# A fixed TensorE order, narrow matmuls gathered into one run per chunk, full-height passes and a reordered front in an mLSTM kernel with attention experts

## The chip, the cores and the metric

The kernel runs on one core of a Trainium2 chip. The metric is device time of one execution in microseconds (us), lower is better. Five engines work side by side: TensorE (PE; its weight loads are shown apart as PEld), VectorE (DVE), ScalarE (ACT), GpSimd (POOL) and SyncE (SP), whose queue issues nearly all DMAs. They wait for each other through semaphores only.

## The reference

Two stages follow each other. The first is an mLSTM with scalar gates for 4 batches x 8 heads, 768 steps, head size 40. The second is a mixture of 4 causal attention experts of size 64 on the result, of which each row uses the best two.

```python
# B, H, S, D = 4, 8, 768, 40
for t in range(S):
    m_new = max(f[t] + m, i[t]); f_stab = exp(f[t] + m - m_new); i_stab = exp(i[t] - m_new); m = m_new
    C = f_stab * C + i_stab * outer(v[t], k[t])
    n = f_stab * n + i_stab * k[t]
    y[t] = sigmoid(o[t]) * (C @ q[t]) / max(abs(n . q[t]), 1)
x = y as (4, 768, 320)
w = softmax of the 2 largest of x @ w_gate, 0 for the others
for e in range(4):
    q, k, v = x @ wq[e], x @ wk[e], x @ wv[e]          # 320 -> 64
    a = softmax(causal(q @ k.T / 8))
    out += w[:, e] * (a @ v @ wo[e])                   # 64 -> 320
```

Inputs and outputs are float32.

## The kernel before

**The mLSTM** is worked in 24 chunks of 128 steps (`chunks`, 6 per batch), each of two halves of T = 64 steps. `gates` (L148) makes the running maxima and cumulated decays of all steps on VectorE with scans. The cumulated log decays G go to DRAM as `gd` and come back, repeated over partitions, as the tile `dm` of each chunk (`load_dm`, L267). For chunk 0 alone (`npe` = 1) PE builds that tile with matmuls of one identity column (L303). `p1_prep` (L281) turns `dm` into the decay matrix with a mask, a bias and an exponential, and makes `ks`, keys times decay, on GpSimd. Then each chunk has four sets of sixteen narrow matmul records, all with 64 or 40 output columns of the array:

- `psc` (L344, `p1_intra`): keys times queries. The queries come as `qbd`, a tile with two heads side by side on a block diagonal, with zeros elsewhere.
- `pdc` (L377, `p1_state`): `ks` times values, the two state increments. VectorE adds them to the decayed state `cd`: `sts` (L402).
- `py` (L409): decayed scores times values.
- `pi` (L424): queries times the states. VectorE then multiplies by exp(G) (`yi`, L434) and adds `py` (L440).

The denominator, the output gate (a tanh) and the product follow on VectorE and ScalarE, and `p1_out` (`px`, L467) transposes the chunk into `xh` and `xl`: a rounded high part for fast passes and the remainder.

Each chunk loads `kqs` (keys and queries, 2 DMAs of 160 KB), `qbd` (2 of 80 KB), `dm` (2 of 128 KB) and `nat` (keys, values, output gate by rows, 648 KB).

**The experts** are worked in 8 units (`units`: batch, half of 384 rows), `part2` at L494. The weights are split into high and low parts too (`split_weights`, L234), so a projection is eight passes (`passes`): high times high, low times high, high times low for the first 256 features, and for the last 64 features one pass over 128 rows (high and low weights stacked) and one pass over 64 rows, `WH[0:64]` with `xl[0:64]`. `queries`, `keys` (L527, 384 columns, four projections a unit) and `values` (L540, 260 columns, three a unit) use them. `queries` writes `QD` and `QL`, `keys` writes `KS`; both go through SP-queue DMAs that copy halves to other partitions.

`scores` (L599) takes, per expert and 128 rows, a pass with `QD` over 128 rows (L611) and a pass with `QL` over 64 rows (L614), in pieces of at most 512 columns. Row block i of half hf has N = (3 hf + i + 1) x 128 columns, so the pieces have 512, 384, 256 or 128 columns: 48, 16, 32 and 32 pairs. VectorE adds the causal mask in place in PSUM and takes the row extreme (L623); ScalarE reads PSUM and writes the exponential to `A` (L633). `flip` (L657) transposes `A` on PE, and ScalarE or VectorE copies it to `AT`. `mix` (L718) multiplies `AT` with the values (64 array columns, L742) and scales by `R`, which goes through DRAM (`fd`). `project` (L758) does the output projection. The last unit works by rows (`flip_rows`, `mix_rows`).

**The order of the work.** Every helper is a generator that yields the estimated PE time of what it has just emitted. `merge` draws from three streams of a unit by weights `ca`, `cb`, `c0`/`c1`: three chunks of the mLSTM six chunks ahead, the next unit's projections, and the unit's scores, flips and mix. A helper can thus be interrupted at each yield: `psc` in four places, `pdc`, `py` and `pi` likewise, and between the passes of a projection. The framework's planner then orders every engine's list by its own estimates and by priorities (`later`, `off`), except where `keep_in_program_order` binds an instruction. The front (from L839) loads chunks 0 to 2 and the weights, keeps PE's clock up with two groups of 16 dummy matmuls (`warm`, L86), and goes through the first five steps of the chunk list before the streams start.

```python
    for n in range(5):
        st = seq1[n][:1] if n == 0 else seq1[n]
        for _ in chain(st):
            pass
```

PSUM has two large buffers (`big`: dummy matmuls and scores) and four of one bank (`one`) for everything else.

## Time and profile before

| | us |
|---|---|
| median of 3 runs | 429.44 |
| lowest and highest of them | 426.6, 430.35 |
| span of the profiled execution, first to last instruction | 430.9 |
| PE busy in it | 406.9 (94%) |
| VectorE, ScalarE, GpSimd busy | 272.4, 199.3, 122.4 |
| mean granted TensorE clock | 0.939 of full |

The profiled execution has no other time of its own than its span, which lies 1.5 us above the median of the runs. The profile's busy time of PE counts matmuls that overlap in a pipeline. How densely they follow each other is read from the starts in the timeline. "Idle before" in brackets is the time that an engine stood still ahead of an instruction, and what ended it.

### The profile page before, as it was taken

The page shows a single profiled execution, that of the slowest core. Times are in us where ns is not written, and L with a number is a line of the kernel's source. Part 1 is how long each engine was busy: PE and PEld are TensorE (multiplying, and loading weights), DVE is VectorE, ACT ScalarE, POOL GpSimd, SP SyncE. Part 2 cuts the span into 40 slices and gives each one's busy share as a digit, 9 for nine tenths or more (in the row PEclk, how much of TensorE's full clock was granted, in tenths as well). Part 3 has the DMA queues.
Part 4 walks back from the last instruction along what each step waited for, and adds up shares of the span by engine and source line. Part 5 has one row for each costly group of instructions (what it writes and reads, how often), then busy time and mean ns, then how long its engine had stood idle before and what let it go on. Part 6 is the DMA issues. An engine that isn't in the chain of part 4 may idle for free.

```text
span 430.9 us, 9143 instructions
## 1 busy us (share of the span) xinstructions
PE 406.9 (94%) x3202; PEld 289.6 (67%) x3202; DVE 272.4 (63%) x844; ACT 199.3 (46%) x561; POOL 122.4 (28%) x157
## 2 busy tenths in 40 slices
PE   6975599899999999999999999999999999989996
PEld 2664478666676776677667767676768766755675
DVE  8686977946967683557746684567766633443552
ACT  1336323434444566336354565344445744543473
POOL 7336533432524523223544043240220000000000
PEclk9785889959989999999999999999999999986999
DMA  6998968755577752446745663255212221420010
GB/s 190 247 223 204 203 187 210 147 150 147 157 192 188 206 153 55 97 138 182 221 95 144 173 185 76 55 185 151 57 42 72 69 56 40 108 65 20 20 44 30
DMA packets 44429, 55.85 MB, mean 130 GB/s; under 512 B 5824, under 2 KB 38816, under 8 KB 44384
## 3 DMA queue, kind: packets, MB, share of 16 engines
q1 hardware_dynamic: 44192, 55.08, 48.7%
q8 instruction: 25, 0.41, 0.4%
q14 instruction: 20, 0.16, 0.1%
q10 hardware_dynamic: 192, 0.20, 0.1%
HBM read 38.59 MB, written 4.07 MB: 99 GB/s over the span
## 4 chain that ended last, share of the span: by engine, by line
PE 81%; DMA 12%; DVE 3%; SPq 1%; ACT 1%; issue 1%; ACTq 0%
PE pp L527 12%; PE sc L614 10%; PE pt L657 10%; PE pa L742 8%; PE sc L611 8%; PE pv L540 7%; PE po L763 6%; PE psc L344 5%; DMA dm<-gd 5%; PE pi L424 3%; DMA qbd<-in_kq 3%; PE py L409 3%; PE pdc L377 3%; DMA kqs<-in_kq 2%; PE pt L679 2%; PE px L467 2%
## 5 line engine op out<-in xcount | busy, mean ns | idle before, releaser
L623 DVE CUSTOM_DVE_ANT_0 sc<-sc,maskw 128x128 f32<-128x128 f32 (+5 forms) x96 | 59.7, 637 | 42.4 <-PE sc L614 38.7
L522 ACT ACTIVATE AT<-pt 128x128 f32<-128x128 f32 (+2 forms) x137 | 49.4, 395 | 53.5 <-PE pt L657 43.5
L633 ACT ACTIVATE A<-sc,nmx 128x128 f32<-128x128 f32 (+5 forms) x96 | 61.0, 636 | 28.0 <-DVE nmx L623 25.5
L611 PE MATMUL sc<-KS,QD 128*128 128x512 f32 (+3 forms) x128 | 52.5, 417 | 1.2 <-ACT A L633 1.1
L614 PE MATMUL sc<-KS,QL 64*128 64x512 f32 (+3 forms) x128 | 53.0, 426 | 0.0
L657 PE MATMUL pt<-cst,A 128*128 128x128 f32 x276 | 48.7, 293 | 0.7 <-DVE dm L356 0.7
L344 PE MATMUL psc<-qbd,kqs 104*64 104x128 f32 x384 | 32.1, 308 | 7.9 <-DMA kqs<-in_kq 3.4
L742 PE MATMUL pa<-AT,V 128*64 128x384 f32 (+2 forms) x240 | 39.1, 423 | 0.0
L657 PEld LDWEIGHTS pt<-cst,A 128*128 128x128 f32 x276 | 31.0, 144 | 11.1 <-issue 2.9
L402 DVE TENSOR_TENSOR sts<-pdc,cd 40x164 f32<-40x164 f32 x80 | 25.9, 324 | 19.2 <-PE pdc L377 18.1
L614 PEld LDWEIGHTS sc<-KS,QL 64*128 64x128 f32 x128 | 23.4, 188 | 21.3 <-issue 15.8
L394 POOL TENSOR_TENSOR cd<-sts,dec 104x328 f32<-104x328 f32 x30 | 22.4, 747 | 52.1 <-DVE sts L402 31.4
L527 PE MATMUL pp<-xl,WH 128*128 128x384 f32 (+1 forms) x96 | 37.0, 385 | 0.0
L527 PE MATMUL pp<-xh,WH 128*128 128x384 f32 x96 | 36.8, 383 | 0.2 <-ACT xh L470 0.2
L611 PEld LDWEIGHTS sc<-KS,QD 128*128 128x128 f32 x128 | 24.4, 194 | 17.9 <-issue 11.5
L756 POOL TENSOR_TENSOR yl<-yf,yh 128x384 fp32r<-128x384 f32 x14 | 14.0, 1003 | 78.9 <-ACT yh L753 78.9
L323 POOL TENSOR_TENSOR dm<-dm,cst 128x512 f32<-128x512 f32 x18 | 23.2, 1290 | 35.9 <-DMA dm<-gd 27.6
L344 PEld LDWEIGHTS psc<-qbd,kqs 104*64 104x64 f32 x384 | 24.2, 152 | 12.8 <-issue 7.5
L742 PEld LDWEIGHTS pa<-AT,V 128*64 128x64 f32 x240 | 18.2, 138 | 14.9 <-issue 12.0
L327 POOL TENSOR_TENSOR ks<-nat,dm 128x320 f32<-128x320 f32 x24 | 18.9, 788 | 27.8 <-PE pdc L377 11.9
L424 PE MATMUL pi<-sts,kqs 104*64 104x82 f32 x384 | 23.4, 249 | 2.6 <-DVE xl L471 1.6
L377 PE MATMUL pdc<-nat,ks 128*40 128x82 f32 x352 | 23.5, 252 | 1.2 <-DVE kl L593 0.9
(133 smaller groups left out, 789.7 us busy)
## 6 DMA issues: line engine op xcount, KB each, us to landing
nat<-in_nat SPq DMA_DIRECT2D x24, 648.0 KB
kqs<-in_kq SPq DMA_DIRECT2D x48, 160.0 KB
QD<-qh SPq DMA_DIRECT2D x64, 96.0 KB
dm<-gd SPq DMA_DIRECT2D x46, 128.0 KB
qbd<-in_kq SPq DMA_DIRECT2D x48, 80.0 KB
out<-ob SPq DMA_DIRECT2D x24, 160.0 KB
KS<-kh SPq DMA_DIRECT2D x32, 96.0 KB
KS<-kl SPq DMA_DIRECT2D x32, 96.0 KB
```

The costliest lines, as they stand in the source:

```text
L344: ins = nc.tensor.matmul(pv[a * T : (a + 1) * T, g, :, sub, :], kc[:, 2 * g + a, sub * T : (sub + 1) * T], qb[:, 2 * g + a, :, sub * T : ( ...
L377: nc.tensor.matmul(pdc[z * 64 : z * 64 + D, o : o + 2 * D1], ks[:, sub, 2 * g + z, :], v1[:, sub, 2 * g + z, :], start=True, stop=True,)
L424: nc.tensor.matmul(piv[sub * T : (sub + 1) * T, g, :, a, :], qc[:, 2 * g + a, sub * T : (sub + 1) * T], sin[sub][:, 2 * g + a, :, :], star ...
L522: nc.scalar.activation(o, x, AF.Copy)
L527: nc.tensor.matmul(pp[:, :HALF], w(slice(mt * P, (mt + 1) * P)), x(slice(0, HALF)), start=(n == 0), stop=(n == len(ps) - 1),)
L540: nc.tensor.matmul(pv[:, : E * HD + E], x(slice(i * P, (i + 1) * P)), w(slice(NQK, NW)), start=(n == 0), stop=(n == len(ps) - 1),)
L611: nc.tensor.matmul(sc[:, o + c0 : o + c1], QDs[p][:, ee, ts], KS[:, e, c0:c1], start=True, stop=False)
L614: nc.tensor.matmul(sc[:, o + c0 : o + c1], QLs[p][r0 : r0 + 64, ts], KS[r0 : r0 + 64, e, c0:c1], start=False, stop=True,)
L623: nc.vector.tensor_tensor_reduce(out=sc[:, o : o + N], in0=sc[:, o : o + N], in1=maskw[:, S - N : S], scale=1.0, scalar=3e38, op0=ALU.add, ...
L633: nc.scalar.activation(A[:, n * HALF : n * HALF + N], sc[:, o : o + N], AF.Exp, bias=nmx, scale=-1.0, accum_out=zs[:, i, e : e + 1],)
L657: nc.tensor.transpose(pt[:, (s - s0) * P : (s - s0 + 1) * P], A[:, c : c + P], ident)
L742: nc.tensor.matmul(pa[ee * 64 : ee * 64 + 64, c0:HALF], kvs[(b, s // 3)][:, s % 3, e * HD : (e + 1) * HD], ATs[e][:, aoff(s) + c0 : aoff(s ...
```

## The change

PE's list is written out by the program and kept (`manual_schedule` for PE); for the front this holds for all engines. The planner's priorities and most of the tuning table go.

- `narrow(n)` emits for one chunk all of `psc` and `pdc` (a new helper `p1_inc`), the `mix` matmuls that stand asked for, and `py` and `pi` of the chunk before, without interruption, then the loads of chunk n+2 and the preparation of chunk n+1. `flow` calls it at even distances of an own clock `clk` and fills the time between with the projections, scores, flips and output projections. A helper that by this clock would still wait for another engine yields `None`, and the next one is taken.
- The `QL` pass and the last `xl` pass of a projection take 128 rows. `QL` becomes a tile per expert with zeros in the other 64 rows, written in two halves by VectorE.
- Queries are multiplied by exp(G) ahead (`p1_scale`, GpSimd). exp(G) goes to DRAM as `ge` and comes back as `eqs` by two DMAs of 96 KB a chunk. `pi` is added to `py` in one bank by PE, and `yi` with its two VectorE operations goes. The denominator starts with an Abs on ScalarE; the copy of the last 64 features moves from GpSimd to VectorE.
- The loads of `kqs` and `qbd` have 48 rows in place of 40: 2 DMAs of 192 and 2 of 96 KB.
- `dm` comes from PE for chunks 0 to 5, with the mask added by PE. For chunks 0 to 2, `qbd` is filled from `kqs` by ScalarE (`spread`) instead of by DMA.
- The masked scores are written to `A` in SBUF, where `exp` works in place. `A` gets four buffers, `ob` three.
- The front: one group of dummy matmuls, gates in three parts between the first chunks, weights behind the loads of chunk 0 to 2, `split_weights` behind chunk 2, then the first two `values` of unit 0. Chunks 3, 4 and 5 come after it.

```diff
+    ctx.enter_context(tc.manual_schedule(engines={mybir.EngineType.PE}))
...
         r += [
             (lambda c: WH[:, 2, c], lambda t: xh[:, 2, t]),
-            (lambda c: WH[0:64, 2, c], lambda t: xl[0:64, 2, t]),
+            (lambda c: WH[:, 2, c], lambda t: xl[:, 2, t]),
         ]
...
+    def p1_scale(b, j):
+        qc = kqs[(b * NCH + j) % len(kqs)][:, 1]
+        nc.gpsimd.tensor_tensor(qc, qc, eqs[(b * NCH + j) % len(eqs)], op=ALU.mult)
...
-        piv = pi[:, : H * D1].rearrange("p (g c a d) -> p g c a d", g=2, c=2, a=2)
+        piv = py[:, : H * D1].rearrange("p (z g a d) -> p g z a d", g=2, z=2, a=2)
         for g in range(2):
             for a in range(2):
-                for sub in range(2):
+                for sub in range(j == 0, 2):
                     nc.tensor.matmul(
                         piv[sub * T : (sub + 1) * T, g, :, a, :],
                         qc[:, 2 * g + a, sub * T : (sub + 1) * T],
                         sin[sub][:, 2 * g + a, :, :],
-                        start=True,
-                        stop=True,
+                        start=False,
+                        stop=g == 1 and a == 1,
                     )
...
-        yi = p2.tile([P, H, D1], F32, tag="yi", name=f"yi_{nm}")
-        nc.vector.tensor_tensor(
...
-        nc.vector.tensor_tensor(yi, pyv, yi, op=ALU.add)
...
         def queries(p):
+            slot = (2 * u + p) % len(qls)
+            while qlu[slot]:
+                yield None
             pq = yield from proj(2 * p)
...
-            nc.vector.scalar_tensor_tensor(QL, pq, -0.125, qh.bitcast(F32), op0=ALU.mult, op1=ALU.subtract)
+            for ee in range(2):
+                r = slice(ee * 64, ee * 64 + 64)
+                nc.vector.scalar_tensor_tensor(
+                    QL[r, ee, :], pq[r], -0.125, qh[r].bitcast(F32), op0=ALU.mult, op1=ALU.subtract
+                )
...
         def scores(es, i):
+            while clk[0] < kr.get((u, es[0] // 2), 1e9):
+                yield None
...
                     nc.tensor.matmul(
                         sc[:, o + c0 : o + c1],
-                        QLs[p][r0 : r0 + 64, ts],
-                        KS[r0 : r0 + 64, e, c0:c1],
+                        QLs[p][:, ee, ts],
+                        KS[:, e, c0:c1],
                         start=False,
                         stop=True,
                     )
...
                 nc.vector.tensor_tensor_reduce(
-                    out=sc[:, o : o + N],
+                    out=A[:, n * HALF : n * HALF + N],
...
+    def narrow(n):
+        c = 0.2
+        if 0 <= n < NC:
+            drive(p1_intra(*chunks[n]))
+            drive(p1_inc(*chunks[n]))
+            c += 1.53
+        for g in asked:
+            c += sum(g)
+        asked.clear()
+        if 3 <= n - 1 < NC:
+            drive(p1_state(*chunks[n - 1]))
+            c += 1.15
+        if 0 <= n and n + 2 < NC:
+            p1_load(*chunks[n + 2])
+        if 0 <= n and n + 1 < NC:
+            p1_prep(*chunks[n + 1])
+            p1_scale(*chunks[n + 1])
+        return c
...
+        while any(x[2] for x in live) or runs or (last and (asked or pend)):
+            if pend and (clk[0] >= pend[0][0] or idle > 20):
+                idle = 0
+                out()
+                continue
+            if (runs and (clk[0] >= nxt or idle > 6)) or (asked and not runs):
+                if pend:
+                    out()
+                idle = 0
+                nxt = run()
+                continue
...
+            st[0] += c
+            clk[0] += c
...
+        drive(p1_intra(0, 0))
+        gates_out(P, 3 * P)
+        decays(0, 6)
         load_weights(0)
...
+        load_weights(1)
+        nc.sync.dma_start(maskf[:, 0:P], const[:, C_MASK:])
+        load_eq(0, 2)
+        load_weights(2)
...
+        split_weights(maskf)
+        nc.sync.dma_start(ge[:, 3 * P : S], g_sb[:, 3 * P : S])
+        for z in range(2):
+            nc.sync.dma_start(gd[:, z * HALF : (z + 1) * HALF], G_sb[:, z * HALF : (z + 1) * HALF])
+        p1_load(0, 3)
...
+        p1_load(0, 4)
+        parts = {0: part2(*units[0])}
+        clk[0] = 2.0
+        for _ in range(2):
+            drive(parts[0][0].pop(0))
```

## Rows read from the trace of the kernel before

**Rows 1.** The page, busy time and share of the span of each engine.
```profile
PE 406.9 (94%) x3202; PEld 289.6 (67%) x3202; DVE 272.4 (63%) x844; ACT 199.3 (46%) x561; POOL 122.4 (28%) x157
```

**Rows 2.** Busy time by stretch; the first row names the columns.
```profile
core 0: us, PE busy (x) PEld busy (x) DVE busy (x) ACT busy (x) POOL busy (x), PEclk, DMA share, GB/s
0.00:55.30 55.30, 39.14 (x373) 28.08 (x373) 42.68 (x99) 19.70 (x60) 28.30 (x37) 0.77 0.87 215
...
84.60:95.00 10.40, 10.39 (x61) 7.48 (x61) 4.59 (x16) 4.12 (x14) 4.50 (x5) 0.51 0.64 161
...
122.30:384.00 261.70, 260.48 (x2008) 184.68 (x2007) 157.47 (x524) 132.25 (x369) 65.21 (x84) 1.00 0.45 121
```

**Rows 3.** Timeline of PE: start, duration, instruction [idle before]; end of the front.
```profile
53.61 1.74 PE L344 MATMUL psc<-qbd,kqs 104*64 104x128 f32 x16 [2.92 <-DMA dm<-gd]
55.28 0.59 PE L540 MATMUL pv<-WH,xh 128*128 128x260 f32 x1
```

**Rows 4.** Timeline of PE at 373 to 381 us: projection and score passes.
```profile
373.50 0.34 PE L527 MATMUL pp<-xl,WH 128*128 128x384 f32 x1
373.68 0.33 PE L527 MATMUL pp<-xh,WH 128*128 128x384 f32 x1
373.94 0.44 PE L527 MATMUL pp<-xl,WH 64*128 64x384 f32 x1
374.31 0.41 PE L763 MATMUL po<-woh,yh 128*128 128x320 f32 x1
...
376.25 0.38 PE L611 MATMUL sc<-KS,QD 128*128 128x256 f32 x1
376.57 0.38 PE L614 MATMUL sc<-KS,QL 64*128 64x256 f32 x1
376.88 0.55 PE L657 MATMUL pt<-cst,A 128*128 128x128 f32 x3
...
379.63 0.49 PE L611 MATMUL sc<-KS,QD 128*128 128x512 f32 x1
380.05 0.50 PE L614 MATMUL sc<-KS,QL 64*128 64x512 f32 x1
380.48 0.33 PE L611 MATMUL sc<-KS,QD 128*128 128x128 f32 x1
380.74 0.32 PE L614 MATMUL sc<-KS,QL 64*128 64x128 f32 x1
380.99 0.43 PE L742 MATMUL pa<-AT,V 128*64 128x128 f32 x2
```

**Rows 5.** The page, costliest groups: score passes, their weight loads, a GpSimd product.
```profile
L614 PE MATMUL sc<-KS,QL 64*128 64x512 f32 (+3 forms) x128 | 53.0, 426 | 0.0
...
L611 PEld LDWEIGHTS sc<-KS,QD 128*128 128x128 f32 x128 | 24.4, 194 | 17.9 <-issue 11.5
...
L323 POOL TENSOR_TENSOR dm<-dm,cst 128x512 f32<-128x512 f32 x18 | 23.2, 1290 | 35.9 <-DMA dm<-gd 27.6
```

**Rows 6.** Timeline of PE at 63 to 65 us: values, then one whole `psc`.
```profile
63.50 0.28 PE L540 MATMUL pv<-WH,xh 128*128 128x260 f32 x1
63.71 0.38 PE L540 MATMUL pv<-WH,xl 64*128 64x260 f32 x1
64.02 1.09 PE L344 MATMUL psc<-qbd,kqs 104*64 104x128 f32 x16
64.94 0.46 PE L377 MATMUL pdc<-nat,ks 128*40 128x82 f32 x8
```

**Rows 7.** Timeline of PE at 201 us: a piece of `psc` between other passes.
```profile
201.25 0.43 PE L344 MATMUL psc<-qbd,kqs 104*64 104x128 f32 x2
201.62 0.55 PE L657 MATMUL pt<-cst,A 128*128 128x128 f32 x3
```

**Rows 8.** Groups of VectorE by line and shape.
```profile
L434 DVE TENSOR_TENSOR yi<-pi,eG 128x328 f32<-128x328 f32 x24 | 11.9, 496 | 7.0 <-PE pi L424 6.6
```

**Rows 9.** Timeline of PE ahead of the slow stretch at 84.6 us.
```profile
84.28 0.33 PE L657 MATMUL pt<-cst,A 128*128 128x128 f32 x1 [0.67 <-DVE dm L356]
```

More of the change, by code (lines that the diff above doesn't have):

```diff
@@ new lines, in mlstm_moe_kernel, with first @@
+    sts = [cp.tile([GR, 4, 2, D1], F32, name=f"sts{i}") for i in range(6)]
+    qls = [cp.tile([P, 2, HALF], F32R, name=f"qls{i}") for i in range(3)]
+    facs = [cp.tile([P, 32], F32, name=f"facs{i}") for i in range(2)]
+    gd = dp.tile([B * H, S], F32, name="gd")
+    ge = dp.tile([B * H, S], F32, name="ge")
+    cN = cp.tile([P, NCH, 2, B, 4], F32, name="cN")
+    gend = gtail.rearrange("p (b j) -> p b j", b=B)
+    dec = cp.tile([GR, 4, B, 2 * NCH], F32, name="dec")
+    loaded = {}
+    def first(b, j):
+        return b == 0 and j < 3
@@ new lines, in load_heads, with spread, load_nat @@
+        return qb, t[:, 0, :, :], t[:, 1, :, :]
+    def spread(b, j):
+        qb, _, qc = loaded[(b, j)][0]
+        for z in range(2):
+            r = slice(z * 64, z * 64 + RP)
+            nc.scalar.activation(qb[r, :, z, :], qc[r], AF.Copy)
+    def load_nat(b, j, t=None, part=None):
+        if t is None:
+            t = ld.tile([P, NNAT], F32, tag="nat", name=f"nat_{b}_{j}", bufs=3)
+        cs = slice(0, NNAT) if part is None else (slice(0, NKV), slice(NKV, NNAT))[part]
+        (nc.sync.dma_start(t[:, cs], nat[b, j][:, cs]))
+        return t
@@ L524, in proj @@
         def proj(mt):
+            while any(clk[0] < xr[(b, hf * 3 + n)] for n in range(3)):
+                yield None
             pp = one(f"pp_{nm}_{mt}")
-            for n, (w, x) in enumerate(ps):
+            for n, (w, x) in enumerate(passes(*xs[(b, hf)])):
                 nc.tensor.matmul(
@@ L802, in part2 @@
[L802 to L828 removed]
+                body.append(scores(*ei[n]))
@@ new lines, in mlstm_moe_kernel, with flow, out, run @@
+    pend = []
+    def flow(runs, streams, gap, first, last=False):
+        live = [[0.0, t, list(items)] for t, items in streams]
+        nxt = clk[0] + first
+        runs = list(runs)
+        idle = 0
+        def out():
+            drive(p1_out(*chunks[pend.pop(0)[1]]))
+            clk[0] += 0.39
+        def run():
+            n = runs.pop(0) if runs else -99
+            clk[0] += narrow(n)
+            if 3 <= n - 1 < NC:
+                pend.append([clk[0] + XD, n - 1])
+            return clk[0] + gap
+        while any(x[2] for x in live) or runs or (last and (asked or pend)):
[6 more added lines that the diff above has]
+                    out()
+                idle = 0
+                nxt = run()
+                continue
+            c = None
+            for st in sorted([x for x in live if x[2]], key=lambda x: x[0] / x[1]):
+                c = next(st[2][0])
+                if c is not None:
+                    break
+            if c is None:
+                idle += 1
+                clk[0] += 0.15
+                assert idle < 200
+                continue
+            idle = 0
+            g = st[2].pop(0)
+            if not isinstance(c, float):
+                asked.append(c)
+                continue
+            c += sum(g)
+            st[0] += c
+            clk[0] += c
@@ L912, in mlstm_moe_kernel @@
+            if tail:
+                streams.append((TW, tail))
+                tot += 2.6
             tail = tl
-        merge(streams)
-    for _ in chain(tail):
-        pass
+        gap = tot / 3
+        flow(runs, streams, gap, gap * NF)
+    flow([], [(1.0, tail)], 9.0, 9.0, True)
 _OUTS = [((B, S, DM), "float32")]
```

631 lines of the change are left out of this document (311 added, 320 removed).

## Prediction

> **What bounds the kernel now.** I read the page's busy times first: TensorE (PE) works 94% of the span, no other engine over 63% [rows 1]. The view of stages then splits this. Up to 55.3 us PE is busy 39 us only, at a granted clock of 0.77, and much of that is dummy work, while the 16 DMA engines are at 0.87 and 215 GB/s: this stretch is bound by loads. From 122 to 384 us PE is busy 260.5 of 261.7 us at full clock with the DMA at 0.45 [rows 2]: here only less PE time helps. The timeline shows where the front ends: the scores of chunk 5 had waited 2.92 us for a `dm` load, and only behind them, at 55.28 us, the first projection pass starts [rows 3].
>
> A busy PE isn't PE at its peak, so the timeline is read by distances from start to start. Inside a projection, 384-column passes over 128 rows follow each other every 0.18 us (373.50 to 373.68). The pass over 64 rows starts 0.26 us after the one before it and is followed only 0.37 us later: 0.63 for two passes that would take 0.36 [rows 4]. The scores alternate 128 and 64 rows all the time: 0.42 and 0.43 us at 512 columns, 0.32 and 0.31 at 256, 0.26 and 0.25 at 128 [rows 4]. The price of a change of the array's shape is thus about 0.09 to 0.2 us on each side, and this kernel pays it in some 300 places for 64-row passes alone (twice 128 score passes, 32 and 24 projection passes).
>
> **The change part by part.** The sum starts from the profiled execution: span 430.9 us; the median of the runs is 429.44, so nothing has to be added around the span and 1.5 us come off at the end.
>
> (a) Score passes over 128 rows. Same-shape passes cost, scaled by columns from 0.176 at 384 [rows 4], 0.235 at 512 and 0.12 at 256; at 128 I take 0.12. Pairs by the code's loops: 48 of 512, 16 of 384, 32 of 256, 32 of 128 columns, 128 in all [rows 5]. Saved per pair: 0.85-0.47 = 0.38; for 384 about 0.37 (between its neighbours); 0.63-0.24 = 0.39; 0.51-0.24 = 0.27. Sum 18.2+5.9+12.5+8.6 = **45 us**. The bound on the small side: if a pass can't be shorter than its weight load (194 ns [rows 5]), the two narrow kinds save 0.24 and 0.12 and the sum is 36. Against that bound: projection passes run at 0.18 with loads of the same length. On the other side, by streaming alone, 50.
>
> (b) The last `xl` pass of the projections over 128 rows: 32 times 0.63-0.36 = 8.6; the values: 0.21+0.31-0.24 = 0.28 [rows 6], 24 times, 6.7. **15 us**.
>
> (c) One run of narrow matmuls per chunk. Narrow (64-column) pieces now start 108 times after 55 us, counted along PE's timeline. Two matmuls of `psc` alone between transposes take 0.37 us [rows 7], while sixteen in a row take 0.92 [rows 6], so two would be 0.12: 0.25 per piece, less where a 64-row neighbour (already counted in a and b) shares it. After the change there are some 27 runs and 6 pieces in the last unit. 75 fewer at 0.15 give **11 us** (7 at 0.09, 19 at 0.25).
>
> (d) The front. Now 215 GB/s times 55.3 us = 11.9 MB come in before the first projection, six chunks among them. The new order wants three chunks (`kqs` 384, `nat` 648, the new `eqs` 192 KB each; `qbd` and `dm` aren't loaded, ScalarE and PE make them), 1.16 MB of weights and some 0.5 MB besides: 5.3 MB, 25 us at that rate. With 3 us to the first packet, the weight split on ScalarE, GpSimd and VectorE behind the last weights (3 to 4 us) and the write of `ge` that the `eqs` loads must read back, I take 34 us (28 if only the loads count, 45 if each of the three `eqs` loads stands 3.5 us in SP's queue with the loads behind it). 21 us earlier. But some three chunks of narrow work move behind the front: sixteen `psc` take 0.92, the other 48 matmuls have 82 columns and by columns 0.6 per sixteen, 2.7 per chunk: 8 back. Net **13 us**.
>
> (e) `dm` from PE for chunks 1 to 5: sixteen narrow records and a mask pass, with two more shapes, 1.6 us by the sixteen `psc` plus three changes; three chunks lie behind the front: **5 us added**.
>
> (f) Costed at nothing. Queries times exp(G) on GpSimd: 128 x 512 there takes 1.29 us [rows 5], 24 times 31 us on an engine that idles 72%; the next chunk's run, over 10 us away, covers it; without cover it is 24 times 1.3 = 31 us. In exchange `yi` (0.5 us, 24 times [rows 8], and its twin that adds) leaves VectorE and `py`/`pi` share a bank. `QL` in two halves adds 16 operations, at the length of `yi` 0.5 us each. The masked score goes to SBUF, and `exp` reads it there: not shown before; taken as 0, bounds -0.1 and +0.1 us on a score group that isn't on PE, which frees the score bank one ScalarE step earlier. DMA per chunk rises from 1384 to 1672 KB from chunk 6 on.
>
> (g) The fixed order adds waits: whatever PE waits for now stands before all that follows in the program, where the planner could put other work first. A score's transposes stand behind VectorE and ScalarE, a chunk's run behind `dm`, `ks` and the states. I take 0: new waits against the half clock that may go (84.6 to 95 us at 0.51, the 1.2 GHz level [rows 2], just behind a gap of 0.67 us in which PE waited for VectorE [rows 9]; at half rate such a stretch costs about half its length, 5 us). Bounds -15 and +25.
>
> Sum: 430.9-45-15-11-13+5 = 352, less 1.5: **350 us**.
>
> The Trainium skill, TensorEngine Tiling (Array Packing), Performance Considerations, speaks against (a): a contraction of at most 64 rows is where two 64-row tiles should be used, for up to twice the speed. Here no two 64-row passes stand next to each other, and each 0.31 to 0.43 us pass runs by itself [rows 4]; by that rule padding gives away half of the passes' array time, by the rows it gives away nothing.
>
> **The rivals.**
> 1. VectorE takes over. Its 272 us lose 24 (`yi`) and some 15 (denominator, decays moved to GpSimd) and gain 8 (`QL`) and 5 (a copy from GpSimd); over 350 us it would be at about 70%, and more in first-half units, where PE's work is least and the three chunks' VectorE work is the same. If every one of the 24 chunk runs waits 1 us for it at the head of PE's order: 350+24 = 374. For: PE does wait for VectorE's `dm` product now and then [rows 9]. Against: from 122 to 384 us VectorE is busy 157 of 262 us [rows 2].
> 2. Nothing new waits, the front ends at 28 us and no half-clock stretch is left behind it: 350-6-12 = 332. For: behind the front PE is idle only 8 of 376 us now (406.9-39.1 busy [rows 1, 2]).
> 3. Slower: loads arrive late at an order that can't go round them. Each run begins with `psc`, which needs `kqs` and `qbd`, and the whole of PE's list stands behind it. The two-chunk lead is about 24 us; with 21% more to load per chunk, and QD, KS and R loads in the same queue, a run that waits over 80/24 = 3.4 us on average eats the gain; 4 us each gives 446. For: such waits of about 3 us are there in the front [rows 3]. Against: the share of 0.45 later [rows 2].
> 4. 64-row passes are the cheap form (the pairing named above) and (a) and (b) turn round: 184 passes of 0.17 us mean, half of it added, 16 us: 430.9-1.5+16-11-13+5 = 426, no change. Against: the distances [rows 4, 6], at each size.
>
> **How the numbers follow.** Forecast, 338 to 364: 0.53. Rival 1, 364 to 424: 0.22. Rival 2, under 338: 0.17. Rival 3: 0.05. Rival 4: 0.03. The range 330 to 378 leaves out the far part of rival 2 and of rival 1, and rivals 3 and 4. A difference of 1% is about what measurement tells from none; faster by over 1%: 0.92, within 1%: 0.03, slower by over 1%: 0.05.
>
> **What would show it.** Right: score pairs 0.23 to 0.24 us apart at 512 columns; `psc` always sixteen in a row; the first `pv` near 34 us with the DMA near 0.9 before it; PE still over 90% busy behind it. Wrong: score passes still 0.4 apart (then (a) is no matter of shape); PE idle before VectorE or a load over 20 us in all behind the front (rivals 1, 3); a first `pv` beyond 45 us.

## The result: 1.2% faster, and the profile after

The changed kernel takes 426.24 us (median of 20 runs), the kernel before 432.37 (20 runs): a ratio of 0.9878, with an interval of 0.9836 to 0.9919. Forecast were 350 us and a range of 330 to 378. The sign was right, the size wrong by 76 us. The executions behind the profiles of the changed kernel (430.4 us) and of e1 below (428.5 us, granted clock 0.791) are among the slower ones of their kernels.

The page of the changed kernel, busy times and the chain that ended last, and under it the chain of the kernel before (PE 81%):

```profile
PE 352.0 (82%) x3234; PEld 293.8 (69%) x3234; DVE 265.2 (62%) x789; ACT 209.9 (49%) x613; POOL 148.6 (35%) x166
...
PE 35%; DMA 21%; DVE 13%; ACT 8%; SPq 8%; issue 7%; POOL 6%; POOLq 0%; ACTq 0%; DVEq 0%
...
PE 81%; DMA 12%; DVE 3%; SPq 1%; ACT 1%; issue 1%; ACTq 0%
```

TensorE lost 55 us of busy time against [rows 1], yet the span is 428.6 us and no other engine is over 62%: nothing took TensorE's place as the engine that is always busy. The chain says the same: 35% of it is PE, where it was 81%, and the rest is spread over DMA, VectorE, ScalarE, GpSimd and SP's queue. Busy time by stretches (columns as in [rows 2]):

```profile
0.00:41.37 41.37, 28.84 (x271) 21.01 (x271) 26.57 (x65) 17.25 (x52) 17.09 (x27) 0.72 0.53 141
41.37:55.60 14.23, 12.34 (x54) 10.59 (x55) 4.84 (x9) 5.75 (x16) 6.26 (x7) 0.50 0.99 252
55.60:120.00 64.40, 50.86 (x551) 44.42 (x551) 47.38 (x142) 27.30 (x91) 34.55 (x42) 0.92 0.76 182
120.00:384.00 264.00, 226.51 (x2093) 191.10 (x2092) 168.26 (x518) 136.09 (x395) 89.72 (x92) 0.94 0.56 146
```

The first projection starts at 41.37 us in place of 55.28, but its stretch up to 55.6 us runs at a granted clock of 0.50. From 120 to 384 us PE is busy 226.5 of 264 us, where it had been busy nearly all of the time [rows 2]: about 37 us of standing still that were not there before.

The timeline of PE (columns as in [rows 3]), at the front, at three gaps, and at score passes:

```profile
34.15 0.87 PE L442 MATMUL px<-cst,xt 128*128 128x128 f32 x3 [4.58 <-DVE xt L426]
...
39.09 0.87 PE L442 MATMUL px<-cst,xt 128*128 128x128 f32 x3 [1.69 <-DVE xt L426]
41.37 0.58 PE L519 MATMUL pv<-WH,xh 128*128 128x260 f32 x1 [1.41 <-ACT WH L253]
...
91.12 1.11 PE L655 MATMUL pt<-cst,A 128*128 128x128 f32 x4 [3.84 <-ACT AT L497]
...
150.61 0.27 PE L604 MATMUL sc<-KS,qls 128*128 128x128 f32 x1
154.60 1.55 PE L655 MATMUL pt<-cst,A 128*128 128x128 f32 x6 [3.71 <-ACT A L625]
155.80 0.67 PE L504 MATMUL pp<-xh,WH 128*128 128x384 f32 x1
156.27 0.52 PE L504 MATMUL pp<-xh,WL 128*128 128x384 f32 x1
156.59 0.52 PE L504 MATMUL pp<-xl,WH 128*128 128x384 f32 x1
...
210.29 0.45 PE L655 MATMUL pt<-cst,A 128*128 128x128 f32 x1 [3.27 <-DVE qls L567]
...
217.57 0.22 PE L601 MATMUL sc<-KS,QD 128*128 128x128 f32 x1
217.63 0.27 PE L604 MATMUL sc<-KS,qls 128*128 128x128 f32 x1
217.74 0.45 PE L601 MATMUL sc<-KS,QD 128*128 128x512 f32 x1
218.03 0.39 PE L604 MATMUL sc<-KS,qls 128*128 128x512 f32 x1
218.26 0.28 PE L601 MATMUL sc<-KS,QD 128*128 128x256 f32 x1
218.38 0.28 PE L604 MATMUL sc<-KS,qls 128*128 128x256 f32 x1
218.50 0.82 PE L655 MATMUL pt<-cst,A 128*128 128x128 f32 x6
...
220.22 1.09 PE L329 MATMUL psc<-qbd,kqs 112*64 112x128 f32 x16
```

The score passes do what was forecast: the low pass is followed after 0.23 us at 512 columns (218.03 to 218.26) and 0.12 us at 256, where [rows 4] had 0.43 and 0.31; `psc` stands as sixteen in a row. The new thing is the brackets of 3 to 4 us. Behind the front there are eight gaps of over 2 us, and each is followed by a stretch at a granted clock of 0.50. So the projection passes at 155.80 to 156.59, behind one of them, follow each other every 0.32 us (after the first), not every 0.18. Over 91 to 96.6 us, behind the gap of 3.84 us, the view of stretches has a clock of 0.50 (the 1.2 GHz level) and PE busy all the same:

```profile
84.00:91.00 7.00, 2.60 (x32) 2.16 (x28) 3.41 (x12) 2.05 (x9) 4.78 (x5) 0.91 0.94 210
91.00:96.60 5.60, 5.48 (x23) 5.10 (x23) 3.33 (x15) 4.01 (x17) 2.73 (x4) 0.50 0.79 206
96.60:104.00 7.40, 7.40 (x89) 6.76 (x89) 6.05 (x18) 4.02 (x13) 4.88 (x6) 1.00 0.49 134
```

**One of these gaps, taken apart.** PE wants `A`, the exponential, from 150.9 us on. Here are ScalarE, then GpSimd, in that stretch:

```profile
153.00 0.63 ACT L311 ACTIVATE dm<-dm 128x512 f32<-128x512 f32 x1 [4.54 <-POOL dm L310]
153.53 0.92 ACT L625 ACTIVATE A<-A,nmx 128x768 f32<-128x768 f32 x1
...
148.62 1.29 POOL L387 TENSOR_TENSOR kqs<-kqs,eqs 112x512 f32<-112x512 f32 x1 [5.47 <-PE pt L655]
150.57 1.26 POOL L309 TENSOR_TENSOR dm<-dm,cst 128x512 f32<-128x512 f32 x1 [0.66 <-DMA dm<-gd]
151.91 1.05 POOL L310 TENSOR_TENSOR dm<-dm,cN 128x512 f32<-128x512 f32 x1
```

VectorE had written the masked scores by 150.7 us. ScalarE stood idle for 4.54 us all the same, since the next chunk's `dm` is ahead of `A` on its list and waited for two GpSimd products; those stood behind a load and behind the product of the queries with exp(G), which is new and had itself waited 5.47 us. (Its bracket names PE; the wait ended when the second `kqs` load, issued at 144.81 us, landed at 148.41.) So the head of PE's list waits for the head of ScalarE's, that for the head of GpSimd's, and that for a DMA. The gaps at 91.12, 185.8 and 280.41 us end the same way, with an operation of ScalarE that stood behind a `dm`, which had waited for GpSimd. The other four of the eight end with VectorE or with another operation of ScalarE.

Over all gaps of PE above 0.15 us behind the first projection, 59 us, ScalarE ended 29 us and VectorE 26, spread over a dozen lines. Such a chain alone doesn't make the difference: e12 below, which hardly waits, has more of ScalarE's waits for the same product. First the changed kernel, then e12:

```profile
ACT dm L311 <- POOL dm L310: 21.5, 12, 4.5
...
ACT dm L329 <- POOL dm L328: 29.0, 15, 3.8
```

(Waits: us in total, times, longest.)

**The account.** For each run the distances from start to start, between pieces (matmuls of one operation in a row), are cut at the median that such a pair of pieces has at full clock; what is left is "work". The excess is "waits" where the clock was full, and "half clock" where it was not. The split is an estimate: another way of cutting moves entries by up to 10 us (e6 and e10 up to 18), and makes the fall in work 56 and the rise of the other two 69; cut matmul by matmul, work is far less and waits far more in every row. All in us, behind the first projection pass:

| run | median | ratio to before (interval) | first projection | work | waits | half clock |
|---|---|---|---|---|---|---|
| before | 432.4 | | 55.3 | 341 | 19 | 12 |
| after | 426.2 | 0.988 (0.984–0.992) | 41.4 | 289 | 69 | 25 |
| e1 | 419.5 | 0.961 (0.953–0.970) | | | | |
| e2 | 394.5 | none given | 51.7 | 289 | 36 | 8 |
| e3 | 458.8 | 1.055 (1.041–1.068) | 41.4 | 345 | 35 | 25 |
| e4 | 409.6 | 0.950 (0.941–0.960) | 40.9 | 284 | 64 | 17 |
| e5 | 442.4 | none given | 42.0 | 283 | 82 | 31 |
| e6 | 419.6 | none given | 41.9 | 289 | 51 | 31 |
| e7 | 424.4 | none given | 41.4 | 284 | 63 | 30 |
| e8 | 397.9 | none given | 51.1 | 284 | 46 | 8 |
| e9 | 436.6 | 1.014 (1.006–1.023) | 41.4 | 285 | 78 | 28 |
| e10 | 422.9 | 0.975 (0.968–0.982) | 42.0 | 283 | 64 | 29 |
| e11 | 408.7 | 0.933 (0.922–0.943) | 41.7 | 290 | 50 | 19 |
| e12 | 382.4 | 0.875 (0.867–0.884) | 51.3 | 287 | 32 | 2 |
| e13 | 397.5 | 0.924 (0.912–0.936) | 43.3 | 292 | 45 | 9 |
| e14 | 425.4 | 0.989 (0.977–1.000) | 54.0 | 286 | 64 | 13 |
| e15 | 387.9 | 0.898 (0.883–0.914) | 50.9 | 286 | 41 | 5 |
| e16 | 389.9 | 0.908 (0.900–0.916) | 50.6 | 284 | 44 | 7 |
| e17 | 388.7 | 0.911 (0.897–0.926) | 50.9 | 288 | 38 | 6 |
| e18 | 423.0 | 0.992 (0.984–1.001) | 41.4 | 283 | 64 | 29 |

The change cut the work by 52 us and started it 14 us sooner; 50 us came back as waits and 13 as half clock. (e1's profile isn't used for the table. One of e2's four runs took 1056.5 us; the other three, 388.8 to 399.6, have a median of 389.5, so what is read against e2 may be 5 us off. The experiments ran on four chips, on which the kernel before had medians of 431.3 to 433.5; the ratios allow for that.)

### The profile page after: what moved, and what is told of

The parts are those of the page before. It is cut to its first block, busy times and chain, and to the rows that moved or that the text cites. A ratio compares the mean times of both kernels' runs of the same rounds, so it can differ in the third digit from the quotient of the medians.

```text
span 428.6 us, 9321 instructions
## 1 busy us (share of the span) xinstructions
PE 352.0 (82%) x3234; PEld 293.8 (69%) x3234; DVE 265.2 (62%) x789; ACT 209.9 (49%) x613; POOL 148.6 (35%) x166
## 4 chain that ended last, share of the span: by engine, by line
PE 35%; DMA 21%; DVE 13%; ACT 8%; SPq 8%; issue 7%; POOL 6%; POOLq 0%; ACTq 0%; DVEq 0%
DMA kqs<-in_kq 7%; PE pa L749 6%; PE pp L504 5%; DMA nat<-in_nat 5%; PE pt L655 3%; DMA eqs<-ge 3%; PE psc L329 3%; ACT A L625 3%; PE po L772 2%; POOL kqs L387 2%; DMA QD<-qh 2%; ACT AT L497 2%; SPq L573 2%; PE pv L519 2%; PE sc L601 2%
## 5 line engine op out<-in xcount | busy, mean ns | idle before, releaser
L625 ACT ACTIVATE A<-A,nmx 128x128 f32<-128x128 f32 (+5 forms) x96 | 63.8, 666 | 14.5 <-DVE nmx L615 13.8
L615 DVE CUSTOM_DVE_ANT_0 A<-sc,maskw 128x128 f32<-128x128 f32 (+5 forms) x96 | 57.3, 618 | 19.8 <-PE sc L604 19.4
L387 POOL TENSOR_TENSOR kqs<-kqs,eqs 112x512 f32<-112x512 f32 x24 | 31.1, 1297 | 54.4 <-DMA kqs<-in_kq 21.6
L601 PE MATMUL sc<-KS,QD 128*128 128x512 f32 (+3 forms) x128 | 46.3, 369 | 2.6 <-DVE nmx L615 2.4
L370 POOL TENSOR_TENSOR cd<-sts,dec 112x328 f32<-112x328 f32 x37 | 27.8, 752 | 43.0 <-DVE sts L378 43.0
L763 POOL TENSOR_TENSOR yl<-R,yh 128x384 fp32r<-128x384 f32 x14 | 14.4, 1027 | 80.8 <-ACT yh L762 61.2
L604 PE MATMUL sc<-KS,qls 128*128 128x512 f32 (+3 forms) x128 | 40.2, 338 | 0.0
L329 PE MATMUL psc<-qbd,kqs 112*64 112x128 f32 x384 | 29.5, 299 | 8.6 <-ACT AT L497 8.6
L504 PE MATMUL pp<-xl,WH 128*128 128x384 f32 x96 | 34.7, 361 | 0.0
L329 PEld LDWEIGHTS psc<-qbd,kqs 112*64 112x64 f32 x384 | 23.2, 148 | 13.9 <-ACT AT L497 10.3
L601 PEld LDWEIGHTS sc<-KS,QD 128*128 128x128 f32 x128 | 25.8, 202 | 6.7 <-DVE nmx L615 4.0
L567 DVE SCALAR_TENSOR_TENSOR qls<-pp,qh 64x384 fp32r<-64x384 f32 x32 | 17.6, 550 | 16.4 <-ACT qh L560 16.2
```

What stands on the lines that cost most here:

```text
L329: nc.tensor.matmul(pv[a * T : (a + 1) * T, g, :, sub, :], kc[:, 2 * g + a, sub * T : (sub + 1) * T], qb[:, 2 * g + a, :, sub * T : (sub + ...
L370: (nc.vector if first(b, j) and sub else nc.gpsimd).tensor_tensor(cd.rearrange("p g z d -> p g (z d)"), sprev.rearrange("p g z d -> p g (z ...
L387: nc.gpsimd.tensor_tensor(qc, qc, eqs[(b * NCH + j) % len(eqs)], op=ALU.mult)
L504: nc.tensor.matmul(pp[:, :HALF], w(slice(mt * P, (mt + 1) * P)), x(slice(0, HALF)), start=(n == 0), stop=(n == 7),)
L601: nc.tensor.matmul(sc[:, o + c0 : o + c1], QDs[p][:, ee, ts], KS[:, e, c0:c1], start=True, stop=False)
L604: nc.tensor.matmul(sc[:, o + c0 : o + c1], QLs[p][:, ee, ts], KS[:, e, c0:c1], start=False, stop=True,)
```

## The experiments

Two bases: the changed kernel with one part undone, and the kernel before with one part done, in which the planner still orders PE.

**e1, the planner's order.** The changed kernel without the hand-written order of PE.

```diff
-    ctx.enter_context(tc.manual_schedule(engines={mybir.EngineType.PE}))
```

> The changed kernel with its one line of fixed TensorE order taken out: the planner orders TensorE's list, everything else stays. Theory F (the fixed list is what costs: it can't go round an instruction that is late, and the same work in another order would have been there): 365 to 395 us, TensorE's idle behind the front falls from 59 to under 25 us. Theory L (loads and the engines behind them come late whatever the order): 415 us or more, and the idle stays over 45 us. Theory P (runs of narrow matmuls are torn apart again and that gives back the gain): shape changes rise from 87 to over 250.

Measured 419.5 us, 2.7% below the changed kernel by the ratios. The fixed order costs 7 us by the medians and 12 by the ratios, and most of the missing 76 is elsewhere. In its profile the gaps of PE that ScalarE ended fall from 29 to 4 us; those that VectorE ended stay, at 29. The largest two:

```profile
PE pt L654 <- DVE sts L377: 9.4, 5, 2.4
PE sc L600 <- DVE nmx L614: 8.4, 11, 1.8
```

**e2, only the full-height passes.** The kernel before, with `QL` as a tile per expert padded by zeros to 128 rows and the last `xl` pass over 128 rows. Two tiles share room with others to make space.

```diff
-            (lambda c: WH[0:64, 2, c], lambda t: xl[0:64, 2, t]),
+            (lambda c: WH[:, 2, c], lambda t: xl[:, 2, t]),
...
-                        QLs[p][r0 : r0 + 64, ts],
-                        KS[r0 : r0 + 64, e, c0:c1],
+                        QLs[p][:, ee, ts],
+                        KS[:, e, c0:c1],
```

> The kernel before with two parts of the change alone: score passes with QL and the last projection pass over 128 rows (QL as three zero-padded tiles; tanh and yf work in place to make room). Order, loads and buffers of before. The prediction's terms a and b are 45+15 us of TensorE time. Theory F: the planner's order keeps TensorE busy, so most of it shows: 370 to 390 us. Theory L or one of other engines' lateness: a TensorE with less work waits just as much: 405 to 425 us, TensorE busy under 88%.

Measured 394.5 us (389.5 without the one run of 1056.5), 38 to 43 below the 432.2 of the kernel before on the same chip, with 52 us less work. This one part does six times what the whole change does.

**e3, the same part undone in the changed kernel.**

```diff
-                        QLs[p][:, ee, ts],
-                        KS[:, e, c0:c1],
+                        QLs[p][ee * 64 : ee * 64 + 64, ee, ts],
+                        KS[ee * 64 : ee * 64 + 64, e, c0:c1],
```

> The changed kernel with the 64-row passes put back (QL and the last xl pass use 64 rows again, about 60 us of TensorE time by the distances in the traces). If the changed kernel is bound by what TensorE waits for, most of the 60 us fall into those waits: 430 to 450 us, TensorE's idle behind the front under 30 us. If TensorE's list is the bound and the waits come on top of it: 470 to 490 us.

Measured 458.8 us, 33 more (29 by the ratios). Its timeline of PE has the old distances back:

```profile
384.26 0.38 PE L601 MATMUL sc<-KS,QD 128*128 128x256 f32 x1
384.57 0.38 PE L604 MATMUL sc<-KS,qls 64*128 64x256 f32 x1
384.88 0.38 PE L601 MATMUL sc<-KS,QD 128*128 128x256 f32 x1
```

0.31 us each, as in [rows 4]. The work rises by 56 us, but 34 us of waits vanish under it: a slower PE hides what it would otherwise stand and wait for. Against the kernel before, e3 has the same work (345 and 341) and is 5.5% slower: the other parts of the change together cost time.

**e4, no chunk loads.** The changed kernel, which from chunk 6 on loads no `kqs`, `qbd`, `eqs` and `nat`.

```diff
+        if n >= 6:
+            t, qb = kqs[n % len(kqs)], qbd[n % len(qbd)]
+            loaded[(b, j)] = (qb, t[:, 0, :, :], t[:, 1, :, :]), last_nat[0], load_dm(b, j)
+            return
```

> The changed kernel with the loads of kqs, qbd, eqs and nat left out from chunk 6 on (the tiles of earlier chunks are used again; the decay tile dm is still loaded), so the output isn't the reference's. Theory L: the waits behind chunk 6 go, 375 to 390 us, and TensorE idles under 25 us behind the front. Theory V (VectorE and ScalarE are late by their own work): 410 to 425 us. Theory F alone (only the order matters): no less than 405 us.

Measured 409.6 us: the loads are worth some 16 us, and 64 us of waits remain without them. The third rival's place was right, its price not.

**e5 and e6, queries not scaled ahead.** `yi` is back on VectorE and GpSimd's product with its loads is gone; e5 in the fixed order, e6 in the planner's.

```diff
-        nc.gpsimd.tensor_tensor(qc, qc, eqs[(b * NCH + j) % len(eqs)], op=ALU.mult)
...
+        nc.vector.tensor_tensor(yi[r], pyv[r], yi[r], op=ALU.add)
```

> The changed kernel with the pre-scaled queries undone: no ge write, no eqs loads (192 KB a chunk), no scaling product on GpSimd (31 us in all); exp(G) comes from transposes on TensorE as before, and VectorE multiplies and adds yi again (24 us more on VectorE). The fixed order stays. Theory S (the scaling step is what makes the chunk late: GpSimd stands in line for the kqs load, behind it the decay tile, behind that ScalarE's copies that free TensorE's transposes): 395 to 412 us. Theory V (VectorE's load makes TensorE wait): slower than the changed kernel, 430 us or more. Theory F (the order alone): within 1% of the changed kernel's 424 us.

> The kernel of e5 with the planner ordering TensorE, so of the change stay the full-height passes, the front, dm from TensorE for six chunks and the smaller buffers. If the fixed order and the scaling step are the two things that eat the gain: 380 to 395 us, as the kernel before with full-height passes alone (394) or better by the earlier front. If the two causes are the same waits seen twice: 400 to 412 us. If the cause lies in what is left (front, buffers, loads): over 412 us.

Measured 442.4 and 419.6 us. Undoing the part doesn't help in either order; in the fixed one it costs 16 us, with more waits (69 to 82): the gaps of PE that VectorE ended grow from 26 to 49 us. That pre-scaling holds up this kernel, by itself, fell here. Beside e5, e6 prices the fixed order once more: 23 us.

**e7, longer latencies in the program's clock.** The order is written from constants of how long the others take; here they are longer.

```diff
-LAG, TW, NF, XD, YD, AD, KD = 2, 5.0, 0.5, 3.2, 2.6, 2.2, 3.5
+LAG, TW, NF, XD, YD, AD, KD = 2, 5.0, 0.5, 5.2, 5.0, 4.2, 5.5
```

> The changed kernel with longer assumed latencies in the program's own clock: chunk to its transposes 5.2 for 3.2 us, mix to output projection 5.0 for 2.6, scores to transposes 4.2 for 2.2, keys to scores 5.5 for 3.5. The order stays fixed, but each follow-up stands further back in the list. If the fixed order is bad because its assumed latencies are too short: 395 to 412 us. If what is late is late by more than any such constant (loads, lists of the other engines): 418 to 430 us. If the list then runs out of other work: over 435 us.

Measured 424.4 us, no difference that counts. Longer constants of this kind don't mend the order.

**e8, whole runs alone.** e2, in which the four sets of a chunk can't be interrupted.

```diff
-                    if a and (g or not PRM['grp']):
-                        yield 0.27 * (1 + PRM['grp'])
...
+        yield 1.08
```

> The kernel of e2 (before, with full-height passes) and no place inside psc and pdc, py, pi of a chunk at which another helper may come between: the runs of the change, but ordered by the planner. Theory P (the change of array shape still costs 0.1 us on each side): shape changes fall from 225 to under 130, 380 to 390 us against 389 to 394 for e2. If long runs make the planner wait for whole chunks: 395 to 410 us.

Measured 397.9 us against 394.5. Shape changes along PE's timeline fall from 225 to 187, work by 5 us, waits rise by 10: nothing gained.

**e9 and e10, the lead given back.** The changed kernel works three chunks beside unit 0 before the next unit; here these are five, so that later units have the old lead, and the runs are spaced for it. e9 in the fixed order, e10 in the planner's.

```diff
-        runs = [n for n in range(3 * k + SH, 3 * k + SH + 3) if n <= NC]
+        runs = [n for n in range(3 * k + 8 if k >= 0 else 3, 3 * k + 11) if n <= NC]
```

> The changed kernel (fixed order) with the mLSTM two chunks further ahead of the experts: chunks 3 to 7 before the first unit's scores instead of 3 to 5, then three per unit, so that a unit's projections find their chunks done a run or two earlier, as in the kernel before. Theory W (what TensorE waits for are the chunk's chain, transposes px and the projections behind it, which the change put one run ahead of their use): 395 to 410 us, and the waits of px, pv and pp on VectorE's xt and xl fall under 8 us. If the lead is not the cause, or five chunks cost in the first unit what they give back later: 420 to 430 us.

> The kernel of e9 with the planner ordering TensorE's list. If lead and fixed order are two causes that add: 385 to 400 us, near e2. If both heal the same waits: 408 to 415 us, as e1 (413 to 415 in its undisturbed runs).

Measured 436.6 us (10 worse than the changed kernel) and 422.9 (3 above e1). A lead doesn't mend it either.

**e11, the lead cut in the kernel before.** e2, with one chunk less ahead of the first unit; a projection there waits until the transposes of its chunk are in the list.

```diff
-    for n in range(5):
+    for n in range(4):
...
-        n0 = 3 * k + 8
+        n0 = 3 * k + 7
```

> The kernel of e2 (before, with full-height passes) with the chunk lead cut by one step to that of the changed kernel: four steps ahead of the streams for five, three chunks per unit from 3k+7, and projections that ask whether their chunk's transposes have been emitted. Theory W: 403 to 420 us, with new waits of px, pv and pp. If the planner makes up for the shorter lead or the shorter front gives it back: 388 to 398 us.

Measured 408.7 us, 14 above e2, although the first projection starts 10 us sooner (41.7 in place of 51.7). The waits behind it rise from 36 to 50 and the half clock from 8 to 19: an earlier start is lost again, and more. (Against 389.5, the median without the one long run, it is 19.)

**e12, fewer buffers.** e2 with two `qbd`, three `dm` and one `R` in place of more.

```diff
-    qbd = [cp.tile([GR, 4, 2, P], F32, name=f"qbd{i}") for i in range(3)]
+    qbd = [cp.tile([GR, 4, 2, P], F32, name=f"qbd{i}") for i in range(2)]
```

> The kernel of e2 with the changed kernel's smaller buffers: two qbd for three, three dm for four, one R for two. If loads that start later are part of the loss: 400 to 410 us. If they don't matter: 388 to 397 us.

Measured 382.4 us, 0.875 of the kernel before (0.867 to 0.884): the best version of this study, faster than both kernels. Its page and the waits of PE:

```profile
PE 342.5 (91%) x3202; PEld 272.8 (73%) x3202; DVE 269.8 (72%) x860; ACT 196.1 (52%) x561; POOL 124.5 (33%) x162
```

```profile
PE psc L348 <- DMA qbd<-in_kq: 4.3, 2, 3.8
PE px L471 <- DVE xt L454: 3.3, 1, 3.3
```

VectorE is busier here than in the changed kernel, 72%, and still no wait for it beyond 3.3 us: a busy VectorE alone doesn't explain the waits of the changed kernel. Why fewer buffers are better was not settled; e2 and e12 differ by 12 us (7 against 389.5) in nothing but buffers, so I read nothing under 10 us between two planner-ordered versions as a cause.

**e13, the lead cut once more,** on e12, by the edit of e11.

> The kernel of e12 with the shorter lead of e11. If starting the projections with one chunk less done is a cause by itself: 10 to 25 us over e12 (392 to 405), the first projection near 42 us for 51, and more waits and half clock behind it, as e11 over e2. If e11's loss was only another plan that came out worse: within 8 us of e12.

Measured 397.5 us: 15 more, as on e2. The lead shorter by a chunk costs about 15 us by itself, on two bases.

**e14 and e17, queries scaled ahead, on e12.** e14 does this part alone; e17 keeps its GpSimd product with a tile of ones and leaves out the loads of exp(G).

```diff
+                nc.sync.dma_start(
+                    eq[z * 64 : z * 64 + D, 2 * x : 2 * x + 2, :],
+                    ge[h : h + 2, j * P : (j + 1) * P][None].to_broadcast([D, 2, P]),
+                )
+        nc.gpsimd.tensor_tensor(qc, qc, eq, op=ALU.mult)
...
-        nc.vector.tensor_tensor(yi, pyv, yi, op=ALU.add)
```

> The kernel of e12 with the pre-scaled queries of the change (exp(G) by DMA, product on GpSimd, py and pi in one bank, no yi on VectorE). If VectorE's list is what TensorE waits for: 370 to 380 us. If the chunk's longer load chain (192 KB more, GpSimd in line for it) costs more: 388 to 405 us. Nothing either way: within 5 us of e12.

> The kernel of e14 (full-height passes, fewer buffers, queries scaled ahead) whose GpSimd product takes a constant tile of ones: the loads of exp(G) are left out, the product and all that it orders stay, so the output isn't the reference's. e14 lies 43 us over e12. If the loads of exp(G) cost that (their place in SP's queue ahead of the next chunks' loads, and 4 MB more), this run comes to 383 to 397 us. If the GpSimd product in the line between a chunk's queries and its matmuls costs it, with the one bank for py and pi, it stays at 415 to 427. Between 397 and 415 both have a part.

Measured 425.4 and 388.7 us. The part costs 43 us on e12. With the product kept and the loads left out, 6 remain by the medians and 16 by the ratios, so the loads are worth 37 or 33 of it, together with the new list that the planner makes for PE in each version; whether the rest is more than two such lists may differ isn't shown. What the loads do stands in the waits of SP's queue in e14, and in its timeline of PE:

```profile
SPq L304 <- POOL kqs L308: 10.4, 7, 2.1
SPq L304 <- DMA nat<-in_nat: 9.0, 7, 2.5
```

```profile
118.45 0.52 PE L474 MATMUL px<-cst,xt 128*128 128x128 f32 x3
129.87 1.98 PE L360 MATMUL psc<-qbd,kqs 104*64 104x128 f32 x16 [10.90 <-DMA eqs<-ge]
```

L304 is the issue of `eqs`: it waits until GpSimd has used the buffer, and all later loads of SP's queue stand behind it (four more issues per chunk, beside). PE then stood 10.9 us for one chunk. In e17 no wait of PE is over 2.3 us:

```profile
PE pt L661 <- DVE xl L471: 2.5, 2, 1.9
PE pt L661 <- ACT ob L770: 2.3, 1, 2.3
```

**e15, `dm` from PE for six chunks,** on e12.

```diff
-PRM.update({... 'npe': 1, ...})
+PRM.update({... 'npe': 6, ...})
```

> The kernel of e12 with dm from TensorE for all six chunks of the first batch (as in the change), which takes ten dm loads out of the front. If the front is bound by loads and an earlier start is kept: 372 to 380 us, first projection before 48 us. If the start comes earlier and is given back in waits behind it: within 5 us of e12. If the added TensorE and VectorE steps show: 386 to 392 us.

Measured 387.9 us, 5 more; the first projection comes 0.4 us sooner. No gain shows from the loads that it saves.

**e16, whole runs,** on e12, by the edit of e8.

> The kernel of e12 with the whole runs of e8 (no place inside a chunk's narrow sets at which other work may come between). If runs are worth their shape changes: 372 to 380 us. If they cost what they save, as e8 against e2: 380 to 392 us.

Measured 389.9 us: again no gain, and waits of 44 us in place of 32.

**e18, the changed kernel without the loads of exp(G),** as e17.

```diff
-                nc.sync.dma_start(
-                    t[z * 64 : z * 64 + RP],
-                    ge[b * H + 4 * z : b * H + 4 * z + 4, j * P : (j + 1) * P][None].to_broadcast([RP, 4, P]),
-                )
```

> The changed kernel whose GpSimd product takes a constant tile of ones: the loads of exp(G) are left out (48 issues of 96 KB, 4.6 MB), the product stays, so the output isn't the reference's. If these loads cost here what they seem to cost under the planner (e14), the time falls by 25 us or more, under 400. If they are a small part of the loads that come late (leaving out all four kinds from chunk 6 on gave 15 us), it falls by 3 to 12 us, to 413 to 422. If the fixed order waits for the product itself or for VectorE, it stays within 3 us of 425.

Measured 423.0 us, 3 less. (The queue's largest wait, for outputs, 37.3 us and 36.6 in e18, lies nearly all behind 387 us and isn't shown.) In the changed kernel the same loads do make SP's queue wait, and it then waits for something else. First the queue of the changed kernel, then of e18:

```profile
SPq L170 <- POOL kqs L387: 28.3, 12, 4.4
SPq L735 <- DVE ft L731: 19.6, 5, 6.3
SPq L130 <- PE py L413: 14.0, 1, 14.0
...
SPq L136 <- PE psc L329: 5.1, 4, 1.5
```

```profile
SPq L728 <- DVE ft L724: 37.6, 10, 6.8
...
SPq L130 <- PE py L406: 21.7, 1, 21.7
SPq L136 <- PE psc L322: 21.4, 7, 5.2
```

The 28 us at `eqs` are gone; `qbd` (L136) now waits 21 us for `psc` in place of 5, `ft` 38 in place of 20. The queue's head has only moved on, to others' results and to buffers that PE's own `psc` frees.

**What stays open.** Under the planner's order the changed kernel stands near 420 us (e1, e6, e10) with the work of e12, which takes 382. No part undone by itself gives the changed kernel more than 16 us (e4). On e12, the shorter lead costs 15 and the scaled queries 43. So the causes seem to cover each other, and a sum over parts undone one by one doesn't close. The waits for ScalarE go in large part with the fixed order (e1: 4 us); those for VectorE, 26 us, stay between 24 and 49 in every version of the changed kernel but e3, and which part of the change makes them was not tried. Nor were all parts undone together, nor the extra buffers of `A`, the 48-row loads, more `dm` from PE or the masked scores in SBUF by themselves.

## Why the prediction was wrong

**Right: the work of PE.** Steps (a), (b), (c), (e) and the 8 us moved from the front say 45+15+11-5-8 = 58 us less behind the first projection; the account has 52 (341 to 289). The distances came out at 0.23 and 0.12 us. Steps (a) and (b) are nearly all of it: e2 alone has 52, e3 gives back 56, and the whole runs of (c) are worth 3 to 5 (e8, e16) once the passes have full height. The bound of 36 us for (a), a pass no shorter than its weight load, fell: 128-column passes follow at 0.06 and 0.11 us (217.57 to 217.74) whose loads are shown with 0.20 us. At 512 columns a pair takes about 0.54 us (the first pass 0.29 to 0.32, the second 0.23) and not the 0.47 of the sum, which is a few of the missing us. The Trainium skill, TensorEngine Tiling (Array Packing), Key Properties, says that a change of the tiling mode drains TensorE; the traces agree, with 0.42 us per 512-column pass where shapes alternate and 0.23 where they don't. Its rule for 64-row contractions (Performance Considerations), as the fourth rival takes it, doesn't hold here for passes that stand alone: e3 pays 33 us for them. That the result lies by the 426 us of that rival is chance.

**Wrong: step (g), the fixed order's new waits, taken as 0 with bounds of -15 and +25.** Measured, waits rose from 19 to 69 us and half clock from 12 to 25: 63 us. Two things were missed. First, the argument that PE was idle only 8 us behind the front holds for a PE with 341 us of work; with 289 it arrives 52 us earlier at others' results, and e3 shows that 34 us of the waits are there or not by PE's speed alone. That speed alone doesn't make them either: e12 has 287 us of work and 32 of waits. Second, the direction of the clock: half clock was to go, and grew, since each of the eight long gaps is followed by a stretch at 0.50. The fixed order itself is 7 to 12 us of it (e1), up to 23 (e5 against e6); the rest is there under the planner's order too, and its cause stays open. Matmuls run strictly in their order, as the Trainium skill has it in TensorE: Matmul & The Clock Gate, Part 3: Packing small matmuls; the trace agrees, since through the 3.7 us before 154.60 no matmul behind the waiting `pt` starts. But e12 with the planner's list, as much in order as any, has 32 us of waits with the same work. So a list in order isn't enough to make the trouble. That what stands at its head does is argued from the gaps above; no run shows it by itself.

**Wrong: step (f), scaled queries costed at nothing.** The product itself was rightly sized (24 times 1297 ns, 31.1 us), and it is covered but for 6 to 16 us (e17). The step counted what GpSimd does and not what the new loads do in SP's queue, whose issues wait for GpSimd in front of the next chunk's loads: 33 to 37 us on e12, with the list that goes with them. In the changed kernel they don't show singly (e18, e5, e6).

**Mis-sized: step (d).** The first projection came at 41.4 us and not at 34, within the bounds of 28 to 45. SP's queue issued no load from 23.4 to 37.6 us, 14.0 us of it one wait of `kqs` (L130) that ended with PE's `py` of an earlier chunk (the weights' loads had been issued by then), and the weights' split on ScalarE then stood behind gates and chunks that waited for each other: PE idles 4.58, 1.69 and 1.41 us. The 3 us to the first packet in the sum is shown by no run (in the kernel before, SP's queue has its first at 1.8 us). Worse, the 14 us gained there were not worth 14: on two bases a lead shorter by a chunk starts 8 to 10 us sooner and ends 15 later (e11, e13).

Together: 63 for (g), of which (f) may be a part, 7 for (d) and 6 for the work are 76 us, the whole miss. That is a sum of what was measured, not of causes shown one by one.

**The rivals.** No engine took over as in the first (VectorE is at 62%, and at 72% in e12, without harm), but its price of 24 us for waits before VectorE was met: 26 us of PE's gaps end with it. The third, loads late at an order that can't go round them, was the nearest in kind and had a chance of 0.05; loads are some 16 us of its price (e4), the rest are chains through VectorE, ScalarE and GpSimd that it didn't name; its average wait comes out at 80/24 = 3.3 us. PE idle over 20 us before VectorE or a load was named as the sign of an error: PE is idle 61 us in all behind the front, 26 of it before VectorE, 29 before ScalarE and next to nothing directly before a load. Two signs of being right failed: the DMA was at 0.53 before the first `pv` and not near 0.9, and PE is busy about 83% behind it and not over 90%.

## What to carry to other kernels

Padding short passes to the shape of their neighbours was worth 38 to 50 us of 432 here (e2, and e12 with fewer buffers) with one operand tile more, so such an edit is tried alone before anything else. When the busiest engine loses some 15% of its work, price the forecast by the next-latest chain and not by zero: follow one result through each queue that it must pass at its head, and count the waits that the slow engine hid. A new load is priced by what stands behind its issue in the queue, not by its bytes, and an earlier start only by what the stages behind it can keep up with.

## What was not expected of the hardware

Two 128-column score passes of one shape take 0.17 us together (217.57 to 217.74), while their weight loads are shown with 0.20 us each (L601, mean 202 ns): neighbours of one shape follow each other that closely, and two shapes side by side take 0.51 [rows 4].

Padding costs TensorE nothing that the traces show: twice the rows, half of them zeros, at 0.23 us for 512 columns, the distance of any full-height pass. VectorE pays for it: `qls` is written by 32 operations of 550 ns, where `QL` took 16 of 555 ns, 8.7 us more.

The gap at 210.29 us ends with VectorE. Two of its operations before it, on 128x12 and 128x9 elements (at 203.03 and 205.45 us), took 2.50 and 2.00 us while GpSimd's products ran; the same kind takes 0.15 to 0.17 us a little later, when GpSimd stands still. Why is not shown.
